# 64 bytes in front of two weight pools: an attention, MLP and mixture-of-experts kernel on one core

## The chip, the cores and the metric

The kernel runs on one core of a Trainium2 chip. The metric is the device time of one execution in microseconds (us), smaller being better. Three runs of the kernel before gave 1903.47 us as their median.

## The reference

Three stages are chained in fp32. Attention pools keys and values by eight, and its result, 2304 tokens of 512 numbers, goes through a wide layer with a cosine gate and then through eight experts that all work on every token, weighted by a matrix that is normalized alternately over rows and columns:

```
x = softmax(scale * q @ pool8(k).T) @ pool8(v)          # -> (2304, 512)
h = x @ w_in;  g = h * cos(h);  x = g @ w_out            # 512 -> 2048 -> 512
P = exp(x @ w_gate - max);  8 times: P normalized over rows, then over columns
out = sum over e of P[:, e] * (relu(x @ w1[e]) @ w2[e])  # 8 experts, 512 -> 1024 -> 512
```

## The kernel before

Every fp32 operand of the large products is split into a high and a low fp32r part, and a product is three matmuls: high by high, high by low, low by high. The tokens are cut into six blocks of 384 (`NB`). In the cosine layer `hidden1` computes 128 hidden features of a block by L989, L990 and L991 (out `ph`), and `output1` sums four of them back into the block by the same lines (out `po`). For the last two blocks the hidden layer is computed by a seven-product scheme (`first_layer`, L1178). The cosine layer ends near 500 us of the span.

The experts are cut into 16 units `u` of 512 hidden features, and the six blocks into three pairs, 48 steps of a unit and a pair in all. Each step has two layers. The **first layer** (`first_layer`, L1178) makes seven products in two halves, so 14 runs of six matmuls, whose moving tile is a piece of the tokens, `xc`, 384 columns wide, and whose stationary tile is a piece of the weights, `whi` or `wlo`. The **second layer** (`strassen_layer`, L1563) has the hidden values `gh` and `gl` stationary and weights `vhi` and `vlo` moving, 256 columns wide, in runs of six or twelve. Between them stand:

```
nc.tensor.matmul(out=ps(), lhsT=l[:, k], rhs=r[:, c, :], ...)    # first layer
nc.tensor.matmul(out=ps, lhsT=l[:, r], rhs=m[:, k], ...)         # second layer
```

`lhsT` is the stationary operand, which a weight load (LDWEIGHTS) brings into TensorE ahead of its matmul, and `rhs` is the moving one. The runs of the second layer of one step are placed among the first-layer runs of the next by a planner that knows the cost of each instruction and not its addresses.

Tiles lie in pools, which are opened in a fixed order by `Group.open`: left pools are stacked upwards from the low end of a partition, right pools downwards from the high end. Where a pool starts therefore follows from the sizes of the pools opened before it. As the program is built, the pools that feed TensorE start as follows, with the remainder by 512 bytes; all slots of these pools, and all slices that a matmul takes of them, are multiples of 512 bytes apart:

```
pool         holds                                     first byte   by 512
xp           moving x of the first layers, gw             2752        192
wp           stationary weights of the first layers,     51904        192
             of hidden1 and of output1
acc0 - acc3  token blocks, sums                          80576        192
gph, gpl     gh, gl                                     118720        448
xq           x of the last two blocks                   137152        448
gbh, gbl     gh, gl                                     149440        448
wq           weights of the cosine layer, seven more    161728        448
tp           scratch tiles r, lt                        176064        448
wp2          moving v of the second layer; in the       199296        128
             cosine layer dhi, dlo (stationary)
```

"Distance" below is the remainder by 512 of the stationary tile's start less the moving tile's start, within a partition.

Of the kernel before, what the change touches and what calls it, by code (L numbers as in the profile page):

```python
# [10 lines left out]
F32 = mybir.dt.float32  # L11
# [12 lines left out]
P = 128  # L24
T = B * S
DM = H * D
KC = DM // P
FU = 512
FC = FU // P
E = 8  # L30
# [3 lines left out]
NT = T // P  # L34
# [6 lines left out]
GW = 32  # L41
# [30 lines left out]
class Group:  # L72
# [9 lines left out]
    def open(self):  # L82
        if self.stack is not None:
            return
        if self.over:
            self.over.open()
        for g in self.after:
            if not g.closed and g.stack is not None:
                g.stack.close()
            g.closed = True  # L90
        self.stack = self.graph.ctx.enter_context(ExitStack())
        if self.name in ("early", "mid"):
            edge = self.stack.enter_context(self.graph.tc.tile_pool(name="edge" + self.name, bufs=1, side=self.side))
            edge.tile([P, 8], F32, name="edge" + self.name)
        for pool in self.pools:
            self.pools[pool] = self.stack.enter_context(
                self.graph.tc.tile_pool(name=pool, bufs=1, side=self.side, reuse_waits="tile"))

# [54 lines left out]
class Graph:  # L153
# [19 lines left out]
    def buf(self, kind, shape, dtype, name):  # L173
        return Buf(kind, shape, dtype, name)
# [274 lines left out]
def fused_kernel(ctx: ExitStack, tc: tile.TileContext, qT, kT, kS, vS, v0, k1, v1, wa1, wb1, wa2, wb2, wg, out):  # L449
# [821 lines left out]
    for u in range(U1):  # L1271
# [16 lines left out]


    gate = {n: buf(k_gc[n], s, F32, n) for n, s in (  # L1290
        ("ones", [P, P]), ("wgr", [P, KC, GW]), ("sel", [P, 6 * E]), ("lg", [P, NT, E]), ("pr", [P, NT, E]))}
    ones, wgr, sel, lg, pr = (gate[n] for n in ("ones", "wgr", "sel", "lg", "pr"))
    add("V", 0.17, lambda: nc.vector.memset(ones.tile, 1.0), [], [ones])
    load(lambda: wgr.tile, lambda: wg, P * KC * GW * 4, writes=[wgr])
# [400 lines left out]
```

## Time and profile before

| | |
|---|---|
| three runs, median (lowest to highest) | 1903.47 us (1903.32 to 1905.5) |
| the profiled execution | 1907.59 us |
| its span, first to last instruction | 1905.9 us |
| TensorE busy, matmuls | 1889.6 us, 99% of the span |
| VectorE, ScalarE, GpSimd busy | 79%, 58%, 19% |
| mean granted clock of TensorE | 0.998 |

Matmuls are pipelined: a matmul's own duration is longer than the time from its start to the next one's start, which is called its pitch below. The pitch is what a stream of matmuls costs, and it is read from the chain of waits (the time a run of six or twelve takes on the chain) or from start times in the timeline.

### The profile page before, as it was taken

What the parts mean: (1) busy time and instruction counts of PE and PEld (TensorE: products, weight loads), DVE (VectorE), ACT (ScalarE), POOL (GpSimd) and SP (SyncE); (2) the same over time, 40 slices, a digit from 0 to 9 for tenths busy, and PEclk for the clock granted to TensorE, in tenths of its full rate; (3) what the DMA queues carried; (4) which work ended last, traced back from release to release, by engine and by line L of the source; (5) the groups of instructions that cost most, each with busy time, mean ns of one, the idle gap of its engine ahead of it and who ended that gap; (6) DMA issues with size and microseconds to landing.
All of it is one profiled execution on the core that took longest, in us unless ns stands there. A gap on an engine that the chain in (4) does not pass through costs nothing.

```text
span 1905.9 us, 33965 instructions
## 1 busy us (share of the span) xinstructions
PE 1889.6 (99%) x13032; PEld 1853.0 (97%) x13032; DVE 1504.0 (79%) x2721; ACT 1102.6 (58%) x2375; POOL 360.7 (19%) x260
## 2 busy tenths in 40 slices
PE   9999999999999999999999999999999999999999
PEld 7789998899999999999999999999999999999998
DVE  7998856987787787778787787877877877878776
ACT  5865434675566665555555565555555565655653
POOL 0213332242102021212122121212121120212120
PEclk9999999999999999999999999999999999999999
DMA  8856662577656556556456465565465564655653
GB/s 267 245 187 238 239 169 71 188 256 263 232 224 254 202 202 262 187 210 243 185 208 257 155 250 212 191 261 198 196 243 194 199 265 160 244 221 191 235 217 116
DMA packets 104762, 406.76 MB, mean 213 GB/s; under 512 B 11160, under 2 KB 15896, under 8 KB 102552
## 3 DMA queue, kind: packets, MB, share of 16 engines
q1 hardware_dynamic: 102616, 400.01, 56.2%
q0 software_dynamic: 1984, 4.59, 1.4%
q8 instruction: 102, 1.67, 0.3%
q14 instruction: 60, 0.49, 0.1%
HBM read 363.40 MB, written 41.16 MB: 212 GB/s over the span
## 4 chain that ended last, share of the span: by engine, by line
PE 93%; DVE 4%; ACT 2%; DMA 1%; issue 0%; SPq 0%; ACTq 0%; DVEq 0%
PE pc L1563 20%; PE py L1178 17%; PE qc L1563 16%; PE px L1178 11%; PE pv L1178 11%; PE po L989 3%; PE po L990 3%; PE po L991 3%; PE ph L989 2%; PE ph L990 2%; PE ph L991 2%; PE px L897 1%; PE ptr L883 0%; DMA wc<-wac 0%; DVE xd L557 0%
## 5 line engine op out<-in xcount | busy, mean ns | idle before, releaser
L1563 PE MATMUL pc<-vlo,gh 128*128 128x256 f32 x1152 | 318.0, 276 | 0.0
L1563 PE MATMUL pc<-vhi,gl 128*128 128x256 f32 x1152 | 318.0, 276 | 0.0
L1563 PE MATMUL pc<-vhi,gh 128*128 128x256 f32 x1152 | 318.0, 276 | 0.0
L1178 PE MATMUL py<-xc,whi 128*128 128x384 f32 x1152 | 293.7, 335 | 0.0
L557 DVE TENSOR_TENSOR gl<-sf,gh 128x384 fp32r<-128x384 f32 x384 | 228.4, 624 | 29.4 <-ACT gh L540 29.2
L540 ACT ACTIVATE gh<-sf 128x384 fp32r<-128x384 f32 x384 | 194.8, 524 | 93.6 <-DVE sf L557 91.5
L1563 PE MATMUL qc<-vhi,gh 128*128 128x256 f32 x864 | 241.7, 280 | 0.9 <-DVE qc L557 0.5
L1563 PE MATMUL qc<-vlo,gh 128*128 128x256 f32 x864 | 239.0, 277 | 0.0
L1563 PE MATMUL qc<-vhi,gl 128*128 128x256 f32 x864 | 238.9, 276 | 0.0
L557 POOL TENSOR_TENSOR raw<-raw 128x512 f32<-128x512 f32 x46 | 60.1, 1307 | 930.3 <-DVE wlo L557 584.4
L1563 PEld LDWEIGHTS pc<-vhi,gh 128*128 128x128 f32 x1152 | 216.3, 188 | 0.1
L1563 PEld LDWEIGHTS pc<-vhi,gl 128*128 128x128 f32 x1152 | 216.3, 188 | 0.0
L1563 PEld LDWEIGHTS pc<-vlo,gh 128*128 128x128 f32 x1152 | 216.2, 188 | 0.0
L1178 PEld LDWEIGHTS py<-xc,whi 128*128 128x128 f32 x1152 | 199.3, 188 | 0.9 <-ACT py L540 0.6
L1178 PE MATMUL px<-xc,whi 128*128 128x384 f32 x768 | 196.5, 336 | 0.0
L1178 PE MATMUL pv<-xc,whi 128*128 128x384 f32 x768 | 196.1, 336 | 0.0
L1178 PE MATMUL py<-xc,wlo 128*128 128x384 f32 x576 | 192.5, 334 | 0.0
L1563 PEld LDWEIGHTS qc<-vhi,gh 128*128 128x128 f32 x864 | 162.1, 188 | 4.6 <-DVE qc L557 0.9
L1563 PEld LDWEIGHTS qc<-vhi,gl 128*128 128x128 f32 x864 | 162.4, 188 | 0.0
L1563 PEld LDWEIGHTS qc<-vlo,gh 128*128 128x128 f32 x864 | 162.1, 188 | 0.0
L1178 PEld LDWEIGHTS px<-xc,whi 128*128 128x128 f32 x768 | 130.1, 188 | 0.6 <-issue 0.6
L1178 PEld LDWEIGHTS pv<-xc,whi 128*128 128x128 f32 x768 | 130.3, 188 | 0.0
(245 smaller groups left out, 4578.6 us busy)
## 6 DMA issues: line engine op xcount, KB each, us to landing
xc<-xc SPq DMA_DIRECT2D x357, 768.0 KB, 6.7
wc<-wac SPq DMA_DIRECT2D x112, 256.0 KB, 4.6
raw<-wb SPq DMA_DIRECT2D x32, 512.0 KB, 7.8
raw<-wa SPq DMA_DIRECT2D x32, 512.0 KB, 4.7
raw<-wa SPq DMA_DIRECT2D x8, 1024.0 KB, 7.2
raw<-wb SPq DMA_DIRECT2D x8, 1024.0 KB, 6.2
wac<-m SPq DMA_DIRECT2D x12, 512.0 KB, 6.3
wac<-cw SPq DMA_DIRECT2D x12, 512.0 KB, 3.7
```

The source lines that it names most:

```text
L540: lambda: nc.scalar.activation(out=out(), in_=in_(), func=func, **{k: v() if callable(v) else v for k, v in more.items()}),
L557: (nc.gpsimd if e == "G" else nc.vector).tensor_tensor(out=out(), in0=in0(), in1=in1(), op=op)
L897: nc.tensor.matmul(out=bank[e * D:(e + 1) * D, off:off + n], lhsT=vs[b][:, 2 * hp + e, :], rhs=pt[:, 2 * hh + e, off:off + n], start=(off ...
L989: nc.tensor.matmul(out=ps, lhsT=lh, rhs=rh, start=(i == 0), stop=False)
L990: nc.tensor.matmul(out=ps, lhsT=lh, rhs=rl, start=False, stop=False)
L991: nc.tensor.matmul(out=ps, lhsT=ll, rhs=rh, start=False, stop=(i == total - 1))
L1178: nc.tensor.matmul(out=ps(), lhsT=l[:, k], rhs=r[:, c, :], start=(start and c + n == 0), stop=(c + n == 3), skip_group_check=True)
L1563: nc.tensor.matmul(out=ps, lhsT=l[:, r], rhs=m[:, k], start=(start and h + n == 0), stop=(h + n == 3), skip_group_check=True)
```

## The change

Where a group is opened, a pool of 64 bytes (16 fp32 numbers per partition) is opened in front of `wp` and another in front of `wq`. Nothing reads or writes them. The tile `sel` of the gate, of which `[:, :E]` alone is used, has `4 * E` columns, not `6 * E`, and so is 64 bytes smaller.

```diff
         for pool in self.pools:
+            if pool in ("wp", "wq"):
+                edge = self.stack.enter_context(self.graph.tc.tile_pool(name="edge" + pool, bufs=1, side=self.side))
+                edge.tile([P, 16], F32, name="edge" + pool)
             self.pools[pool] = self.stack.enter_context(
                 self.graph.tc.tile_pool(name=pool, bufs=1, side=self.side, reuse_waits="tile"))
...
-        ("ones", [P, P]), ("wgr", [P, KC, GW]), ("sel", [P, 6 * E]), ("lg", [P, NT, E]), ("pr", [P, NT, E]))}
+        ("ones", [P, P]), ("wgr", [P, KC, GW]), ("sel", [P, 4 * E]), ("lg", [P, NT, E]), ("pr", [P, NT, E]))}
```

In the built program `wp`, the four `acc` pools, and the gate's `wgr` and `sel` start 64 bytes later (remainder 256), `wq` and `tp` start 64 bytes later (remainder 0), and every other pool stays where it was: the smaller `sel` takes back the bytes in front of `wp`, and free space behind `tp` takes those in front of `wq`. The instructions of every engine stand in the same order as before, with the same sizes. One wait is added: since a slot of `gbl` now also overlaps the sixth slot of `wq`, one early VectorE instruction of the experts (`gl<-sf,gh`) also waits for the transfer that had last filled that slot. The distances change so:

```
matmuls                                   stationary  moving    before  after
expert first layer, L1178                 wp          xp          0       64
hidden1, output1 and P1, P2, P4           wp          xp          0       64
  of L1178 in the cosine layer            wq          xp        256      320
                                          wp          xq        256      320
                                          wq          xq          0       64
                                          wp          gph, gpl  256      320
                                          wq          gph, gpl    0       64
other L1178 of the cosine layer           wp2         xp        448      448
  (dhi, dlo)
expert second layer, L1563                gph, gbh,   wp2       320      320
                                          gpl, gbl
last matmul of a first-layer run, with    gph, gbh    xp        256      256
  the next load for the second layer
last matmul of a second-layer run, with   wp          wp2        64      128
  the next load for the first layer
```

## Rows read from the trace of the kernel before

**Rows 1.** The page: span, TensorE's busy time, shares of the chain of waits.
```profile
span 1905.9 us, 33965 instructions
PE 1889.6 (99%) x13032; PEld 1853.0 (97%) x13032; DVE 1504.0 (79%) x2721; ACT 1102.6 (58%) x2375; POOL 360.7 (19%) x260
...
PE 93%; DVE 4%; ACT 2%; DMA 1%; issue 0%; SPq 0%; ACTq 0%; DVEq 0%
```

**Rows 2.** Windows: stretch, length, busy us and instructions by engine, clock, DMA.
```profile
150.00:540.00 390.00, 386.46 (x2304) 372.81 (x2303) 301.02 (x514) 216.57 (x408) 114.08 (x75) 1.00 0.61 208
540.00:1880.00 1340.00, 1339.62 (x9697) 1336.09 (x9696) 1052.96 (x1951) 773.89 (x1718) 229.27 (x164) 1.00 0.56 216
```

**Rows 3.** Chain of waits inside the experts: start, us, engine, tile, line, matmuls.
```profile
1003.40 1.06 PE px L1178 x6
1004.46 1.04 PE pv L1178 x6
1005.50 0.68 PE qc L1563 x6
1006.18 1.04 PE py L1178 x6
1007.23 1.36 PE pc L1563 x12
1008.59 1.05 PE px L1178 x6
1009.64 1.04 PE py L1178 x6
1010.68 0.68 PE qc L1563 x6
```

**Rows 4.** Timeline of the cosine layer, TensorE: start us, us, instruction.
```profile
203.98 0.33 PE L991 MATMUL ph<-xh,wc 128*128 128x384 f32 x1
...
205.20 0.33 PE L989 MATMUL po<-gh,wc 128*128 128x384 f32 x1
...
207.97 0.33 PE L990 MATMUL po<-gl,wc 128*128 128x384 f32 x1
```

**Rows 5.** Timeline, TensorE: the cosine layer's products with dhi and dlo.
```profile
421.87 0.51 PE L1178 MATMUL pv<-xP,dhi 128*128 128x384 f32 x2
...
423.95 0.35 PE L989 MATMUL po<-gw,wc 128*128 128x384 f32 x1
```

**Rows 6.** Timeline, TensorE: three matmuls of 512 columns, merged.
```profile
502.79 0.86 PE L1149 MATMUL pset<-xc 128*128 128x512 f32 x3
```

**Rows 7.** The tile pset: duration ns (min/median/max) of the same three.
```profile
L1149 PE MATMUL pset<-xc x3: 390/397/397, 502.8 to 503.3; 128*128 128x512 f32 x3
```

**Rows 8.** Groups of instructions: TensorE matmuls with whi, and with wc at L1178.
```profile
L1178 PE MATMUL py<-xc,whi 128*128 128x384 f32 x1152 | 293.7, 335 | 0.0
...
L1178 PE MATMUL px<-xc,whi 128*128 128x384 f32 x768 | 196.5, 336 | 0.0
L1178 PE MATMUL pv<-xc,whi 128*128 128x384 f32 x768 | 196.1, 336 | 0.0
...
L1178 PE MATMUL px<-xx,wc 128*128 128x384 f32 x96 | 19.1, 335 | 0.0
...
L1178 PE MATMUL py<-xP,wc 128*128 128x384 f32 x48 | 9.8, 339 | 1.2 <-ACT r L540 0.7 <-DVE c L557 0.6
```

**Rows 9.** Groups of instructions: a weight load of the first layer.
```profile
L1178 PEld LDWEIGHTS py<-xc,whi 128*128 128x128 f32 x1152 | 199.3, 188 | 0.9 <-ACT py L540 0.6 <-DVE c L557 0.3
```

**Rows 10.** Windows of line L989 alone: stretch, length, TensorE busy us (matmuls).
```profile
150.00:372.00 222.00, 123.00 (x360) 0.99 0.56 177
372.00:510.00 138.00, 46.28 (x138) 1.00 0.68 244
```

**Rows 11.** The tile wc: its loads on SyncE's queue, first and last issue.
```profile
L562 SPq DMA_DIRECT2D wc<-wac x112: 319/383/1317, 85.8 to 463.9; - x112
DMA to landing us min/median/max: 2.5/4.6/8.4
```

**Rows 12.** Timeline, VectorE: the instruction that gets one more wait.
```profile
518.12 0.59 DVE L557 TENSOR_TENSOR gl<-sf,gh 128x384 fp32r<-128x384 f32 x1
```

## The prediction

> **What bounds the kernel now.** I began with the page: TensorE has matmuls in flight for 99% of the span and holds 93% of the chain of waits [rows 1]. The windows then show where it does not wait: from 540 to 1880 us it is busy for 1339.62 of 1340 us while VectorE is busy for 1053 us, or 79%, and from 150 to 540 us for 386 of 390 us [rows 2]. So behind 150 us each nanosecond of a matmul's pitch is a nanosecond of the kernel, and no other engine stands close behind. The third view is the chain inside the experts, which gives pitches: a second-layer run of six takes 0.68 us and one of twelve 1.36 us, 113.3 ns a matmul; a first-layer run of six takes mostly 1.04 us, 173.3 ns a matmul [rows 3]. [...]
>
> **What goes with the excess.** Every narrow matmul behind those 113.3 ns has distance 320, or 64 where a first-layer load is next. The wide ones have other distances, and all the same pitch: in the cosine layer, at distances 0 and 256, 23 matmuls from 203.98 to 207.97 us give 173.5 ns [rows 4]; at distance 448, 12 matmuls from 421.87 to 423.95 us give 173.3 ns [rows 5]. A weight load takes 188 ns [rows 9], longer than either pitch, so it always runs beside the matmul ahead of it, and the two read the same partitions at once. That is the mechanism I suppose: where the load's lines and the moving tile's lines fall on the same part of the memory at the same time, the stream loses a few cycles, and at 64 or 320 it does not. The trace cannot prove it, since width and distance never vary apart: no wide matmul has a distance of 64 or 320 and no narrow one another. But after the change nearly all wide matmuls have one of these two.
>
> **The change part by part.** No instruction is added, removed or moved; addresses alone change.
>
> *The price of one wide matmul at 64 or 320.* The trace has no such row, so I bound it. [...] Lower gain: three matmuls of 512 columns at distance 0 take 0.86 us, of which the last one is 397 ns [rows 6, 7], so two pitches are 463 ns and one is 231.5 ns; from 384 to 512 columns a column costs (231.5 - 173.3) / 128 = 0.455 ns, and 113.3 + 128 x 0.455 = 171.5 ns, 1.8 ns less. I take the narrow matmul in proportion, 113.3 x 384 / 256 = 170.0 ns, **3.33 ns less**; it lies between the two and nearer to the slope that rows show. Nothing gained, and a loss, are rivals below.
>
> *How many.* In the experts the three rows with `whi` are 1152 + 768 + 768 = 2688 matmuls, and each run has four of these and two with `wlo`, so 4032 matmuls in 672 runs [rows 8]. The last matmul of a run that a second-layer run follows is read beside a load of `gh` at distance 256, as before; in the chain that is 3 of 5 runs [rows 3], so about 403 keep their pitch and 3629 change. In the cosine layer L989 has 360 + 138 = 498 matmuls behind 150 us [rows 10], and L990 and L991 as many each, 1494; with the 96 + 48 at L1178 that use `wc` [rows 8] that is 1638. Together 5267. Those before 150 us (attention is woven in there, and TensorE waits for it) I leave out.
>
> *The sum.* 5267 x 3.33 ns = 17.6 us. The profiled execution's 1907.59 us would become 1890.0 us. It stands 4.1 us above the median of the three runs, which is what I predict: 1903.47 - 17.6 = **1885.9 us**.
>
> *What I cost at nothing, or nearly.* The 403 narrow matmuls that a first-layer load follows go from distance 64 to 128, which no row shows. They could gain nothing and lose at most the same 3.33 ns, 1.3 us in all. VectorE's and ScalarE's tiles in `acc` and `tp` move by 64 bytes; in the experts VectorE has 287 us to spare in 1340 [rows 2] and can hide a few per cent. The added wait is for a load of `wc`: the last was issued at 463.9 us and the slowest landed after 8.4 us [rows 11], 46 us before the waiting instruction starts at 518.12 us [rows 12]. Faster first-layer runs ask VectorE and ScalarE for results 20 ns a run sooner; TensorE's idle time of 0.4 us in 1340 says that there is room.
>
> **Rivals.**
>
> *A. The excess hangs on width alone.* [...] For it: 0, 256 and 448 all give 173.3 ns, so three distances made no difference. [...] The change would then do nothing: 1903.5 us.
> [...]
>
> [...]
> [...]
>
> *C. It is slower: 64 is the wrong distance for a wide stream.* A stream of 384 columns runs on for a third of its time after the narrow one would have ended, and the load that follows may then start at another moment of it. [...] It decides as soon as a first-layer run takes more than 1.04 us. Against it: a load of `wp` beside a narrow stream at distance 64 costs nothing that the chain shows, as runs of L1563 in front of L1178 still take 0.68 us and 1.36 us [rows 3].
>
> **How the numbers follow.** Forecast (170.0 ns, between 1.8 and about 4.5 ns saved, 1880 to 1894 us): 0.57. B: 0.11. A: 0.20. C: 0.12. About 0.2%, 3.8 us, is what a measurement of this kernel can tell from no change. Faster is the forecast and B, 0.68; same is A, 0.20; slower is C, 0.12. The range from 1866 to 1905 us takes in the forecast, B's value with 2 us below it, and A's value; it leaves out C and some of the scatter. The forecast's own range is 1880 to 1894 us.
>
> **What would show it.** Right: first-layer runs of about 1.02 us in the chain, second-layer runs still 0.68 us, L989 to L991 near 170 ns from start to start, the products with `dhi` and `dlo` still at 173.3 ns, and the last matmul of a run before a second-layer run still at 173 ns. [...] Wrong in another way: if first-layer runs shrink and TensorE's idle time behind 540 us grows above a few us, the gain went into waits for VectorE.

## The result and the profile after

The changed kernel takes **1928.97 us** (median of four runs, 1927.04 to 1930.53) against 1903.72 us before (1903.32 to 1905.5), a ratio of 1.013 with a 95% interval of 1.0115 to 1.0145. It is slower by 25 us where 17.6 us of gain had been forecast.

The page of the changed kernel, its span, busy times and chain of waits, answers to [rows 1] (its lines stand three further down in the file: L1563 is L1566, L1178 is L1181):

```profile
span 1928.7 us, 33965 instructions
...
PE 1913.3 (99%) x13032; PEld 1878.3 (97%) x13032; DVE 1507.7 (78%) x2721; ACT 1103.8 (57%) x2375; POOL 355.6 (18%) x260
...
PE 93%; DVE 4%; ACT 2%; issue 0%; DMA 0%; SPq 0%; POOL 0%; ACTq 0%
```

TensorE is as busy as before and the clock is granted as before (0.999 of full speed, before 0.998). No wait has come: the windows, which answer to [rows 2], show 1339.62 of 1340 us busy again, but with 9540 matmuls in that stretch, not 9697.

```profile
150.00:540.00 390.00, 388.17 (x2312) 374.34 (x2311) 302.62 (x514) 216.04 (x408) 112.88 (x75) 1.00 0.62 208
540.00:1880.00 1340.00, 1339.62 (x9540) 1337.53 (x9539) 1042.24 (x1928) 766.93 (x1698) 225.36 (x164) 1.00 0.56 213
```

So matmuls have become dearer, and the chain of waits inside the experts tells which. It answers to [rows 3]:

```profile
1004.19 1.04 PE pv L1181 x6
1005.24 0.71 PE qc L1566 x6
1005.94 0.71 PE pc L1566 x6
1006.65 0.71 PE qc L1566 x6
1007.36 0.71 PE pc L1566 x6
1008.07 1.04 PE py L1181 x6
...
1014.03 1.04 PE py L1181 x6
1015.07 1.42 PE pc L1566 x12
```

The first-layer runs, whose own distance is the one that changed, still take 1.04 us. The second-layer runs take 0.71 and 1.42 us in place of 0.68 and 1.36, 118 ns a matmul in place of 113.3, though neither their stationary nor their moving tiles have moved; of their distances only the one beside the load of `wp` at a run's end is another. The groups of instructions say the same in the mean duration of one matmul, first before:

```profile
L1563 PE MATMUL pc<-vhi,gl 128*128 128x256 f32 x1152 | 318.0, 276 | 0.0
```

and after, where the first layer's 335 ns is that of [rows 8]:

```profile
L1566 PE MATMUL pc<-vhi,gl 128*128 128x256 f32 x1152 | 324.8, 282 | 0.0
...
L1181 PE MATMUL py<-xc,whi 128*128 128x384 f32 x1152 | 293.4, 335 | 0.0
```

In the cosine layer, which answers to [rows 4], 23 matmuls from start to start take 4.02 us, 174.8 ns each where they took 173.5:

```profile
203.89 0.34 PE L992 MATMUL ph<-xh,wc 128*128 128x384 f32 x1
...
207.91 0.34 PE L994 MATMUL po<-gh,wc 128*128 128x384 f32 x1
```

Added up over all starts in the two traces: the 6048 matmuls of the second layer take 716.7 us where they took 691.3, 25.4 us more; the 4032 of the first layer 701.6 us where they took 704.4, 2.8 us less; the 1494 of L989 to L991 behind 150 us 0.9 ns each, 1.3 us more. Together that is 24 us; the spans of the two traced executions differ by 22.8 us.

**What the trace of before already held.** Here is its chain of waits 3 us ahead of [rows 3]:

```profile
1000.23 1.05 PE py L1178 x6
1001.28 0.71 PE qc L1563 x6
1001.99 0.71 PE pc L1563 x6
1002.69 0.71 PE qc L1563 x6
```

These are second-layer runs at 118 ns, at the distance of 320 that I had called free. I counted them from the starts of all matmuls: call a stretch of second-layer matmuls between two others a run, and count it as one at 118 ns when the median pitch in it is above 115.5 ns, else as quick. Before, 26 of 427 runs are at 118 ns; after, 412 of 427. Hardly any lies between: before, 401 runs have a median of 113 or 114 ns, 24 one of 117 to 119, and two one of 116. Of the 26 runs at 118 ns before, 19 are entered over a pitch of 190 ns or more, that is, after a short stall (the one shown is not), where only 3 of the 401 quick ones are; of the 15 quick ones after, 13 come after a pitch of 140 ns or more.

The trace of before also has a change of pace inside a run. Of its 15 runs of thirty matmuls, 14 stall ahead of the 25th, where two pitches of 190 to 194 ns follow each other. The 23 pitches ahead of them have a median of 113 ns, the four behind them one of 116.5 to 118 ns, at the same distances. Here is one of them:

```profile
711.78 0.28 PE L1563 MATMUL pc<-vlo,gh 128*128 128x256 f32 x1
711.89 0.28 PE L1563 MATMUL pc<-vhi,gl 128*128 128x256 f32 x1
712.08 0.36 PE L1563 MATMUL qc<-vhi,gh 128*128 128x256 f32 x1
712.27 0.28 PE L1563 MATMUL qc<-vlo,gh 128*128 128x256 f32 x1
712.39 0.28 PE L1563 MATMUL qc<-vhi,gl 128*128 128x256 f32 x1
712.51 0.28 PE L1563 MATMUL qc<-vhi,gh 128*128 128x256 f32 x1
712.63 0.28 PE L1563 MATMUL qc<-vlo,gh 128*128 128x256 f32 x1
712.74 0.28 PE L1563 MATMUL qc<-vhi,gl 128*128 128x256 f32 x1
```

This gave the theories that were tested.

- **H**: the second layer has two paces at the same addresses. Which one a run has hangs on the moment at which weight loads and the moving stream meet when it is entered, and it keeps it to its end. F is its rival: addresses fix the pace.
- For what decides the moment: **P**, the first layer's own distance (0 before, 64 after); **X**, the distance at the end of a second-layer run, where the first layer's load meets the narrow stream (64 before, 128 after); **O**, the other tiles that moved.

### The profile page after: what moved, and what is told of

Read it like the earlier page. It is cut to its first block, busy times and chain, and to the rows that moved or that the text cites. A ratio compares the mean times of both kernels' runs of the same rounds, so it can differ in the third digit from the quotient of the medians.

```text
span 1928.7 us, 33965 instructions
## 1 busy us (share of the span) xinstructions
PE 1913.3 (99%) x13032; PEld 1878.3 (97%) x13032; DVE 1507.7 (78%) x2721; ACT 1103.8 (57%) x2375; POOL 355.6 (18%) x260
## 4 chain that ended last, share of the span: by engine, by line
PE 93%; DVE 4%; ACT 2%; issue 0%; DMA 0%; SPq 0%; POOL 0%; ACTq 0%
PE pc L1566 21%; PE py L1181 17%; PE qc L1566 16%; PE pv L1181 11%; PE px L1181 11%; PE po L992 3%; PE po L994 3%; PE po L993 3%; PE ph L992 2%; PE ph L993 2%; PE ph L994 2%; PE px L900 1%; PE ptr L886 0%; ACT r L543 0%; DVE xd L560 0%; DVE r L1014 0%
## 5 line engine op out<-in xcount | busy, mean ns | idle before, releaser
L1566 PE MATMUL pc<-vhi,gl 128*128 128x256 f32 x1152 | 324.8, 282 | 0.0
L1566 PE MATMUL pc<-vhi,gh 128*128 128x256 f32 x1152 | 323.7, 281 | 0.0
L1566 PE MATMUL pc<-vlo,gh 128*128 128x256 f32 x1152 | 323.5, 281 | 0.0
L1181 PE MATMUL py<-xc,whi 128*128 128x384 f32 x1152 | 293.4, 335 | 0.0
L1566 PE MATMUL qc<-vhi,gh 128*128 128x256 f32 x864 | 244.8, 283 | 0.9 <-DVE qc L560 0.5
L1566 PE MATMUL qc<-vhi,gl 128*128 128x256 f32 x864 | 243.1, 281 | 0.0
L1566 PE MATMUL qc<-vlo,gh 128*128 128x256 f32 x864 | 242.4, 281 | 0.0
L1566 PEld LDWEIGHTS pc<-vlo,gh 128*128 128x128 f32 x1152 | 220.6, 192 | 0.0
L1566 PEld LDWEIGHTS pc<-vhi,gh 128*128 128x128 f32 x1152 | 216.2, 188 | 0.1
L1566 PEld LDWEIGHTS pc<-vhi,gl 128*128 128x128 f32 x1152 | 216.2, 188 | 0.0
L1181 PEld LDWEIGHTS py<-xc,whi 128*128 128x128 f32 x1152 | 200.4, 188 | 0.9 <-ACT py L543 0.6
L1181 PE MATMUL px<-xc,whi 128*128 128x384 f32 x768 | 195.7, 336 | 0.0
L1181 PE MATMUL pv<-xc,whi 128*128 128x384 f32 x768 | 195.4, 335 | 0.0
L1181 PE MATMUL py<-xc,wlo 128*128 128x384 f32 x576 | 193.5, 336 | 0.0
L1566 PEld LDWEIGHTS qc<-vhi,gh 128*128 128x128 f32 x864 | 162.2, 188 | 3.2 <-DVE qc L560 0.9
L1566 PEld LDWEIGHTS qc<-vlo,gh 128*128 128x128 f32 x864 | 164.5, 190 | 0.0
L1566 PEld LDWEIGHTS qc<-vhi,gl 128*128 128x128 f32 x864 | 162.2, 188 | 0.0
L1181 PEld LDWEIGHTS px<-xc,whi 128*128 128x128 f32 x768 | 131.1, 188 | 0.6 <-issue 0.6
L1181 PEld LDWEIGHTS pv<-xc,whi 128*128 128x128 f32 x768 | 131.3, 188 | 0.0
```

What stands on the lines that cost most here:

```text
L1181: nc.tensor.matmul(out=ps(), lhsT=l[:, k], rhs=r[:, c, :], start=(start and c + n == 0), stop=(c + n == 3), skip_group_check=True)
L1566: nc.tensor.matmul(out=ps, lhsT=l[:, r], rhs=m[:, k], start=(start and h + n == 0), stop=(h + n == 3), skip_group_check=True)
```

## The experiments

For each kernel the table has the three distances ("first": first layer; "end": load of wp beside the last narrow matmul of a run; "entry": load of gh beside the last wide one), the quick runs of 427, the mean pitch of the second and of the first layer in ns without stalls (pitches above 140 and above 200 ns are left out), all from the starts in the trace, and the time. The second layer's own distance is 320 in all. Where no number of runs is given, the time is that of a single run; runs of the kernel before beside these gave 1899.4 to 1908.7 us, so a few us between two single runs tell nothing, and the pitches are the evidence there.

```
                         first end entry  quick second first   us
before                      0   64   256   401   113.5  174.3  1903.7 (4 runs)
after                      64  128   256    15   118.0  173.6  1929.0 (4 runs)
e1 wp alone                64  128   256    13   118.0  173.6  1928.8
e2 wq alone                 0   64   256   411   113.4  174.3  1906.3
e3 xp 64 lower             64   64   320   372   114.0  173.1  1903.4
e9 the same, timed         64   64   320   392   113.9  173.1  1901.8 (11 runs)
e4 xp and wp higher         0  128   192   197   115.9  175.9  1924.4
e7 wp by 128              128  192   256   188   115.9  176.0  1927.0
e8 wp by 32                32   96   256     7   117.7  174.9  1931.3
e12 all but xp by 32       32   64   288    10   117.7  174.2  1927.9
e13 and xp 64 lower        96   64   352     4   117.6  173.5  1927.9
e14 all by 64               0   64   256   423   113.4  174.2  1903.1
e15 all but xp by 64       64   64   320   380   113.9  173.1  1903.3
e16 and xp 64 lower       128   64   384   251   115.1  176.4  1924.2
e5 after, 8 columns        64  128   256   203   116.5  173.8  1919.9
e6 after, 16 columns       64  128   256   239   116.2  174.2  1920.7
e11 after, 8 in all        64  128   256   365   114.5  173.9  1911.1 (8 runs)
e10 before, 8 columns       0   64   256   291   114.7  175.1  1914.0
```

**e1 and e2: the two halves of the change**

```diff
-            if pool in ("wp", "wq"):
+            if pool == "wp":
```

> The padding in front of wp alone (wq and tp stay where they were). What the traces of before and after show: the second layer, whose own addresses did not move, went from 113.3 to 118 ns a matmul, a state that before shows too, in 26 of its 427 runs. Theory P: the first-layer stream's own distance (now 64) leaves the weight loads and the moving stream in another phase to each other, and the second layer keeps it; then second-layer pitch 118 ns and about 1929 us. Theory X: what decides is the last matmul of a second-layer run, beside a load of wp at distance 128 instead of 64; also 118 ns, about 1929 us. Theory O: the move of wq and tp did it; then 113.3 ns and about 1904 us, or in between.

e2 has `pool == "wq"` and `sel` as before.

> The padding in front of wq alone, sel as before. P and X: the experts keep 113.3 ns and the time is 1904 us within 2 us (the cosine layer uses wq at distances 320 and 64 in places). O: 118 ns in the second layer and up to 1929 us.

e1 has the whole loss (1928.8 us, 13 quick runs), e2 none of it in the experts (411 quick runs). O fell. What e2 shows in the cosine layer is 174.7 ns a matmul for L989 to L991 where before has 173.7: with `wq` at 64 and 320, the distances that were to make them faster, they are 1 ns slower.

**e3 and e4: one of the two distances at a time**

```diff
-    warm = const.tile([P, 16], F32, name="warm")
...
+            if pool == "wp":
+                edge = self.stack.enter_context(self.graph.tc.tile_pool(name="edge" + pool, bufs=1, side=self.side))
+                self.graph.warm = edge.tile([P, 16], F32, name="warm")
```

> wp and all behind it stay as before; xp starts 64 bytes lower, since the small tile warm moves from in front of xp to in front of wp. First-layer distance 64 as in the change; a load of wp beside the narrow stream keeps distance 64 as before; a load of gh beside the last wide matmul goes from 256 to 320. P: second layer at 118 ns, about 1929 us. X: second layer at 113.3 ns, about 1903 us or a little less.

e4 is the change with the pool of 64 bytes in front of `xp` alone.

> xp and wp both 64 bytes higher: first-layer distance 0 as before, a load of wp beside the narrow stream at distance 128 as in the change, a load of gh beside the last wide matmul at 192. P: second layer at 113.3 ns, about 1904 us. X: second layer at 118 ns, about 1930 us.

The first layer at 64 with the old distance at the end has 372 quick runs: P fell as it stood. At 0 with 128 at the end, 197 runs are quick. That spoke for X, as a tendency.

e4 shows something else besides. Its first layer has the distance 0 of before and takes 1.6 ns a matmul more, all of it in the runs that follow a second-layer run:

```profile
1007.31 1.06 PE px L1181 x6
1008.37 1.04 PE pv L1181 x6
```

Over the trace the runs behind a second-layer run take about 1.06 us and those behind a first-layer run 1.04. So the wide stream, too, can go at more than one pace at one and the same distance, by what it follows.

**e5, e6, e10 and e11: the moment alone, no address**

```diff
-                            nc.tensor.matmul(out=ps(), lhsT=l[:, k], rhs=r[:, c, :], start=(start and c + n == 0),
+                            wide = banks is None and name in ("P1", "P5", "P2", "P3") and (
+                                c + n == 3 or start and c + n == 0)
+                            nc.tensor.matmul(out=bank[:, :NB + 8] if wide else ps(), lhsT=l[:, k],
+                                             rhs=xb[0].tile.rearrange("p a b n -> p (a b n)")[:, c * NB:(c + 1) * NB + 8]
+                                             if wide else r[:, c, :], start=(start and c + n == 0),
```

The eight more columns land behind the 384 in the bank and nothing uses them. The runs that write `py` are left as they are and serve as the control within the same kernel. e5 is the changed kernel with this edit; e6 has 16 columns in place of the eight.

> [...] No address changes. Theory H (the second layer has two paces at the same addresses, 113.3 and 118 ns, and keeps the one in which a run was entered): second-layer runs entered behind px and pv change their pace in part, those behind py stay at 118 ns; the time falls below 1929 us if 8 columns are the right shift. Theory F (the pace is fixed by the addresses in use, whatever the moment): 118 ns everywhere, and the time about 2 us up, from some 960 matmuls x 3.3 ns = 3 us.

> [...] H: again a change of pace behind px and pv, with another share than at 8 columns, or none if 16 columns are a whole period. F: 118 ns everywhere and the time 5 to 7 us up.

The chain of waits of e5 (L1183 is the first layer, L1570 the second):

```profile
1006.92 1.04 PE pv L1183 x6
1007.96 0.69 PE qc L1570 x6
1008.65 1.04 PE py L1183 x6
1009.68 1.42 PE pc L1570 x12
1011.10 1.04 PE px L1183 x6
1012.15 1.04 PE py L1183 x6
1013.18 0.71 PE qc L1570 x6
1013.89 0.71 PE pc L1570 x6
1014.60 1.04 PE pv L1183 x6
1015.65 0.68 PE qc L1570 x6
1016.33 0.68 PE pc L1570 x6
```

Behind `pv` the second layer takes 0.68 or 0.69 us again, behind `py` still 0.71 and 1.42. Over the whole trace 135 of 137 runs behind `pv` are quick and 45 of 49 behind `px`, but 19 of 235 behind `py`; after the change alone it was 1, 9 and 1. The kernel computes more columns (576 matmuls are wider, not the 960 of the expectation), and yet its second layer takes 708.3 us for 716.7; the single run is 9 us quicker than the median of the changed kernel. No run shows the 3.3 ns that the expectations of e5 and e11 set for eight columns; at the 0.455 ns a column that [rows 3], [rows 6] and [rows 7] give I estimate 3.6 ns, 2.1 us for the 576. F fell, and H holds as far as pitches show it: with every start address the same, eight columns at the end of one matmul change the pace of the six or twelve that follow, behind `pv` from 1 quick run of 137 to 135. The meeting of load and stream itself no run shows. At 16 columns the picture is another one (93 of 137 behind `pv`, 3 of 49 behind `px`), and 139 of 235 behind `py`, where nothing was widened. These are all the 139 whose `py` run follows a widened one, and none of the 96 whose `py` run follows the second layer: the shift is handed on through a run of six unshifted matmuls.

> The 8 columns of e5 (runs that write px and pv alone) in the kernel before, whose second layer runs at 113.3 ns. H: the shift can throw a good entry as well as mend a bad one, so some of the second-layer runs behind px and pv go to 118 ns, those behind py stay at 113 ns. F, or a gain that 8 columns bring by themselves: 113.3 ns everywhere, time up by 3 us for the columns.

The same eight columns in the kernel before, its chain of waits (L1180 first layer, L1567 second):

```profile
1006.42 1.05 PE py L1180 x6
1007.47 1.36 PE pc L1567 x12
...
1012.28 1.05 PE pv L1180 x6
1013.33 0.71 PE qc L1567 x6
1014.04 0.71 PE pc L1567 x6
1014.75 1.04 PE py L1180 x6
1015.79 1.05 PE px L1180 x6
1016.84 0.71 PE qc L1567 x6
```

Here they spoil it: 44 of 137 runs behind `pv` and 11 of 49 behind `px` are quick (137 and 34 before), and 234 of 235 behind the untouched `py`. So the columns are neither good nor bad in themselves; that it is the moment which counts is my reading of these numbers.

e11 widens the runs that write `py` too (and the ScalarE copy that opens `py`).

> The changed kernel with the last matmul 8 columns wider in all first-layer runs of the experts, py included (the copy that opens py is 8 columns wider too). H with e5's result: behind py as behind px and pv nine second-layer runs in ten at 113.3 ns, so that the 25 us of the second layer come back, less 3 us for about 770 matmuls x 3.3 ns and 2 us for the loads of wp at distance 128: 1906 to 1911 us. If the runs behind py differ in kind: 1917 to 1922 us as e5.

365 runs are quick and the time is 1911.07 us, a ratio to before of 1.003 (1.002 to 1.0041), so 18 to 20 of the 25 us come back without a tile moved. What stays are the columns themselves (864 matmuls, not the 770 of the expectation; at my estimate of 3.6 ns each they are 3.1 us), 62 runs at 118 ns, and the loads of `wp` at distance 128: in e11 the narrow matmul beside such a load takes 117.9 ns on the mean, in the change 121.4, before 113.6.

**e7 and e8: other paddings**

```diff
-                edge.tile([P, 16], F32, name="edge" + pool)
+                edge.tile([P, 32], F32, name="edge" + pool)
```

> 128 bytes in front of wp alone, sel 128 bytes smaller: first-layer distance 128, load of wp beside the narrow stream at 192, load of gh beside the wide stream at 256. X in its narrow form (only a load that meets the narrow stream at 64 mod 256 is free) says that 192 is as bad as 128: second layer near 118 ns, 1920 to 1930 us. If only 128 is bad: 113.3 ns and about 1904 us.

e8 has `[P, 8]`.

> 32 bytes in front of wp alone, sel 32 bytes smaller: first-layer distance 32, load of wp beside the narrow stream at 96. If lines of 64 bytes are what counts, a start in mid-line is like one of its two neighbours, 64 or 128: 1904 or 1929 us; in between otherwise.

Neither is as good as no padding. e7 is a mixture, which neither of its two expectations had, and e8 is nearly all at 118 ns, like the change.

**e12 to e16: is it the distance at the end?**

In e12 and e13 all pools but `xp` move 32 bytes up; in e14 to e16 64 bytes.

```diff
-        if self.name in ("early", "mid"):
+        if self.name == "early":
...
+            if pool == "wp":
+                edge = self.stack.enter_context(self.graph.tc.tile_pool(name="edge" + pool, bufs=1, side=self.side))
+                edge.tile([P, 8], F32, name="edge" + pool)
```

For 64 bytes, two one-column tiles of the normalization (`m1`, `nm`) share a tile besides, which moves the right end by the 32 bytes that are still wanted. In e13 and e16 `xp` is lower as in e3; in e14 the padding stands in front of `xp`.

> All pools of the experts but xp 32 bytes higher (32 bytes in front of wp, the 32 bytes of padding at the right end left out): first-layer distance 32 as in e8, load of wp beside the narrow stream at 64 as before (96 in e8), load of gh beside the wide stream at 288 (256 in e8), second layer's own distance 320. X (the distance at the end of a second-layer run, where the first layer's load meets the narrow stream, picks the pace): 113 to 114 ns, 1900 to 1907 us. P (the first-layer distance picks it): 117.7 ns as in e8, about 1930 us.

> As e12 with xp 64 bytes lower besides: first-layer distance 96, load of wp beside the narrow stream at 64, load of gh beside the wide stream at 352. X: 113 to 114 ns, 1900 to 1907 us. If the distance at the entry of a second-layer run (352, or 288 in e12) has a say of its own, the two differ, and one of them is slow.

> Every pool that TensorE reads in the experts 64 bytes higher, xp too: all distances as before (first layer 0, end of a second-layer run 64, its entry 256), all starts moved. If distances alone count: 113.3 ns, 1903 to 1907 us. If the absolute start counts (e12 and e13 had gh, vhi and wp start in mid-line, 32 past a multiple of 64, which this one avoids): another pace.

> As e14 with xp where it was: first layer 64, end of a run 64, entry 320, the distances of e3. Distances alone: as e3, 113 to 114 ns in most runs, 1900 to 1905 us. Absolute starts: otherwise.

> As e15 with xp 64 bytes lower: first layer 128, end of a run 64, entry 384. X without mid-line starts: 113 to 114 ns, 1900 to 1907 us. If the first layer's distance or the entry picks the pace: near 118 ns or a mixture as in e7, 1915 to 1930 us.

X fell: in e12 and e13 the distance at the end is the old one and nearly every run is at 118 ns, and in e16, with starts on multiples of 64, 251 are quick and the first layer is slow in its own right. e14 and e15 settle another point: with every start moved by 64 bytes and the distances of before the experts are those of before (423 quick runs), and with those of e3 they are e3's (380 and 372). In these, distances count and absolute starts don't. Whether a start 32 bytes past a multiple of 64, as `wp`, `gh` and `vhi` have it in e12 and e13, has a say of its own was not tested. e15 also answers a rival from the change itself, that of the `acc` pools, which move along with `wp`: in it `xp`, `wp` and `acc` start where the changed kernel has them, of the tiles that TensorE reads in the experts those of the second layer alone are 64 bytes higher, and 380 runs are quick where the change has 15. No single one of the three distances picks the pace: 64 in the first layer, 64 at the end and 256 at the entry each stand in a good set and in a bad one. Kernels with the same set agree (before, e2 and e14; after and e1; e3, e9 and e15). Only the distances of before and those of e3 were good.

**e9: a version a little faster than before**

> The kernel of e3 timed. Its first look had second-layer runs mostly at 113 ns and the first layer at 173.2 ns a matmul for 174.2 before, which should be 4032 x 1.0 = 4 us less, and 3 us more in the second layer (55 slow runs for 26). H: within 2 us of before, rather below it: 1901 to 1904 us. If single looks differ by more than that, no difference can be told.

1901.76 us (11 runs), a ratio of 0.9983 (0.9974 to 0.9992) to 19 runs of the kernel before beside it. Its chain of waits:

```profile
1003.55 1.04 PE px L1181 x6
1004.59 1.04 PE py L1181 x6
1005.63 0.68 PE qc L1566 x6
1006.31 0.68 PE pc L1566 x6
1006.99 1.04 PE pv L1181 x6
1008.03 0.68 PE qc L1566 x6
```

The first-layer runs here take 1.04 us: over the whole trace 645 of 672 do, where before 240 do and 394 take 1.05. (So the 1.04 us that the prediction read as usual in [rows 3] was the smaller part.) All of the first layer takes 699.6 us for 704.4, 4.8 us less, of which the second layer's 693 to 694 us for 691.3 give about 2 back. What is gained lies at the seam: in before, the first two matmuls of a run that follows the second layer take 175 and 179 ns, here 170 and 173; behind the first two both have a median of 173.

## Why the prediction was wrong

**What bounds the kernel** was right: TensorE almost without waits from 150 us on, before and after (386.46 and 388.17 us busy of 390 up to 540 us, 1339.62 of 1340 behind), and 24 us of pitch came with 22.8 us of span.

**The price of a wide matmul at 64** was the step that carried the sum, "3.33 ns less", and it failed. Inside first-layer runs the pitch is 173.4 ns at distance 64 and 173.6 at 0, with the same median of 173; over all of the first layer it fell by 0.7 ns, from its seams. With the cosine layer's 1.3 us more, 1.5 us came in place of the 17.6. So the 3.33 ns that I read as the wide matmul's excess and as a price of distance 0 (173.3 ns for 170.0, the narrow matmul in proportion) were not one: at 64 the wide pitch stands as it stood, as rival A had it. The 170.0 ns were an estimate, and no run shows the wide stream at that pitch: the lowest mean of the first layer is 173.1 ns (e3, e9 and e15). The confounding was named (width and distance never vary apart in the trace), but the forecast still gave the distance 0.57.

**"Lose at most the same 3.33 ns, 1.3 us in all"**, the bound for the narrow matmuls that go to distance 128, failed too, and it is the step that gave the loss. Those 424 take 121.4 ns for 113.6, which is 3.3 us; and what they and the seams hand on had no term in the sum at all. The other 5600, at unchanged addresses and unchanged distances, take 118 ns for 113.5, 22 us.

**The rivals.** A was right about the first layer and wrong about the time, as nothing in it touched the second layer. That no address matters, which A would come to, is not borne out: e14 and e12 should then have one pace, and they have 113.4 and 117.7 ns. Whether the weight load is what takes the time, no run shows. B's value, 2 us above the lower end of the range, needed a wide stream quicker still than 170.0 ns, and no run shows that either. C was right that it is slower, but not where: its mark, first-layer runs above 1.04 us, was not seen in the change, though distance 128 shows it (e7 and e16: 1.05 and 1.06 us, 176 ns a matmul, behind either layer). Its reason against itself, that runs of L1563 ahead of L1178 still took 0.68 us, was true of the trace and said nothing of another distance.

**The test of the mechanism** in the trace of before was there to be made: runs at distance 320 that take 0.71 us, 2 us ahead of the rows that I chose, and runs that change from 113 to 118 ns behind a stall. They say that a distance does not fix a pace.

What was not settled: why a set of distances gives the one moment or the other. The three that were varied are tied (entry = 320 + first - end at this second-layer distance), so the entry was never varied alone, and no run shows the reads themselves. That two reads meet in the memory stays an inference from the pitches.

## What to carry to other kernels

When TensorE has no waits (here 1339.62 of 1340 us busy), read the pitch of its matmuls run by run and not as a mean: two paces at the same addresses, here 113 and 118 ns, were the sign that runs keep what they were entered with, as 406 of 427 did before. A shift of tiles by 64 bytes then has to be judged on all streams that follow one another, not on the one that it moves, and tried rather than reasoned; here two sets of distances in nine were good. Widening the last matmul of a run by a few unused columns is a cheap test for it, since it moves no address: eight columns took the quick runs of 427 from 15 to 203 in e5 and from 401 to 291 in e10.

## What was not expected of the hardware

- A stream of 256-column fp32r matmuls runs at 113.3 or at 118 ns, with the same tiles and the same granted clock (1.00 from 540 to 1880 us, before and after), and mostly stays at it for a run of six to thirty. Of the 427 runs of before 21 change it inside: 14 go from 113 to 118 ns behind a stall, and seven begin slower and settle at 113 ns after about six matmuls.
- Eight more columns at the end of the matmul ahead, 392 for 384, put 135 of 137 runs behind `pv` into the faster pace in the one layout (e5) and 93 of 137 into the slower one in the other (e10).
- A stall goes with the same: pitches of 190 ns and more at the entry with 19 of the 26 runs at 118 ns before, and pitches of 140 ns and more with 13 of the 15 quick ones after.
- 384 columns have a median pitch of 173 ns inside runs at first-layer distances 0, 32, 64 and 96 (before, e12, after, e13), and 173.3 to 173.5 ns in the cosine layer at 0, 256 and 448; but 175 ns at 128 (e7, e16), and a mean of 177 ns at 0 where the runs follow the second layer in e4.
